# Linear attention and two mixer blocks in fp32 on one core: the main part of the first MLP taken from 288-token halves to block products over 256 and 512 tokens, with six early hidden tiles instead of five

## The chip, the core and the metric

The kernel runs on one core of a Trainium2 chip. The time is the device time of one execution in microseconds (us); of several runs the median is given. The engines are TensorE (PE; its loads of weights are PEld), VectorE (DVE), ScalarE (ACT), GpSimd (POOL) and SyncE (SP), whose queue issues the transfers (DMA). Each engine goes through its own instructions in order and waits for the others by semaphores.

## What is computed

Four batches of 576 tokens with 512 channels go through a linear attention with 8 heads and then through two mixer blocks:

```python
num = np.einsum('bhsf,bhfd->bhsd', q_p, kv)          # q_p, k_p = phi(q), phi(k)
x   = (num / den) as (batch, 576, 512)
u   = x + ((x.T @ U) @ V).T                          # mixing 1 over tokens, rank 32
x2  = u + relu(u @ w_ch1) @ w_ch2                    # first MLP, 512 -> 2048 -> 512
u2  = x2 + (relu(x2.T @ w_tok1) @ w_tok2).T          # mixing 2 over tokens, 576 -> 256 -> 576
out = u2 + relu(u2 @ w_m1) @ w_m2                    # second MLP, 512 -> 1536 -> 512
```

All of it is fp32. PE works on pairs of fp32r numbers: each operand is split into a high part (cast on ACT) and a low part (the difference, on DVE or POOL), and each product is the sum of three matmuls (high·high, high·low, low·high).

## The kernel before

The program has three stages, one after the other on PE, and the work around them overlaps.

The **attention stage** (to 394.8 us) goes through 16 groups of a batch and two heads in an order written out by hand (`rounds`, filled by `at`). Between them stand matmuls of the first MLP as a fill: NA = 5 of its 16 hidden tiles (a tile is 128 hidden channels), for 8 half batches of 288 tokens (hp_a is the first product, yp the second; their results go to DRAM as sD, u itself as uD). At its end come the mixing 1 of the last batch (rp, then mp) and the last halves' fill.

The **middle stage** (394.8 to about 741 us) does the other 11 hidden tiles for the same 8 halves (`channel`): per tile and half 12 matmuls of 288 columns into hp_b, a relu split (`relu_split`: hh on ACT, then hl on DVE), and two tiles later 12 matmuls into yb. The weights arrive as words of 64 bits that ACT and DVE decode (raw_b to w_b); the second MLP's words (raw_c) are decoded beside it and written back to DRAM as wD. After two halves follows `tokmix2`, mixing 2 of that batch: transposes x2p, the first product gp, a relu split (gh, gl), the second product m2p in four PSUM buffers. It is added to x2 in place and u2 goes to DRAM.

The **last stage** (from about 741 us) is the second MLP, 12 hidden tiles as 6 pairs, over token chunks c0 to c4 of 256, 512, 512, 512 and 512. c0 takes plain products. In the others `seven` computes a pair's first product as seven block products (Strassen's scheme, in Winograd's form): 2 × 2 blocks of the weights (sh, sl, 7 matrices, of which `sums` forms four) and of the tokens (`token_mats`, t0 to t6), 42 matmuls of 256 columns into PSUM tiles x, y, z, v instead of 48 of 512 columns at half the count. `second` then adds 24 matmuls of 512 columns a pair. x and y share two PSUM buffers (psh): x of the next pair waits until both readers of this pair's x are done. Its weights are loaded from wD, cast and split.

Of the kernel before, what the change touches and what calls it, by code (L numbers as in the profile page):

```python
# [19 lines left out]
P = 128  # L20
# [12 lines left out]
NA = 5  # L33
NR = NF2 - NA
# [4 lines left out]
READY = 8  # L39
FIRST = (4, 3, 5, 6, 2, 1, 0, 7, 8, 9, 10)  # L40
# [12 lines left out]
RAWX = 3  # L53
# [31 lines left out]
LAG = 2  # L85
O_WA = 4
D_WA = 5
# [8 lines left out]
def body(ctx, tc, kq, vd, w_phi, U, V, wm1, wt1, wt2, wm2, out):  # L96
# [32 lines left out]
    uD = [dr.tile([P, NC, N], F32, name=f"uD{i}") for i in range(2 * B)]  # L129
    sD = [dr.tile([P, NC, N], F32, name=f"sD{i}") for i in range(2 * B)]  # L130
# [230 lines left out]
    def split_tokens(xp, pool, nm, t):  # L361
        xh = pool.tile([P, C], F32R, tag="xh", name=f"xh{nm}")
        if t == 4:
# [101 lines left out]
    def tm2(b, ch):  # L465
# [10 lines left out]
        nc.sync.dma_start(uD[2 * b + ch], xT[:, :, sl])  # L476
# [56 lines left out]
    def ma_y(b, ch, c):  # L533
# [10 lines left out]
        if c == NC - 1:  # L544
            nc.sync.dma_start(sD[2 * b + ch], ys.pop((b, ch)))
# [76 lines left out]
    wB, begun = {}, []

    def load_next():
        f = FIRST[len(wB)]
        wB[f] = load_b(f)

    def half_next():
        f, k = FIRST[len(begun) // 2], len(begun) % 2
        if f >= NR:  # L630
            return
        begun.append(k)
        if k == 0:
            wB[f] = w_tiles(wrB[f], f"b{f}", f)
        load_half(wm1, NA + f, f"b{f}", k, *wB[f])
# [5 lines left out]
    while len(begun) < 2 * NR:  # L641
        half_next()
    while len(wB) < READY:
        load_next()
    PS.close()
    PB = ExitStack()
    psh = ctx.enter_context(tc.tile_pool(name="psh", bufs=2, space=PSUM, reuse_waits="tile"))
    psy = ctx.enter_context(tc.tile_pool(name="psy", bufs=1, space=PSUM, reuse_waits="tile"))
    psg = PB.enter_context(tc.tile_pool(name="psg", bufs=1, space=PSUM, reuse_waits="tile"))

    words = [(f, k) for p in range(NF2 // 2) for k in range(2) for f in (2 * p, 2 * p + 1)]

    def decode():
        f, k = words.pop(0)
        sl = slice(k * C, (k + 1) * C)
        nc.sync.dma_start(wD[f][:, sl], load64(wm2[f][:, sl], P, C, f"c{f}_{k}"))

    def channel(fs, uh, ul, xc, u, nm, pool=mlp):
        n = uh.shape[2]
        yp = [psy.tile([P, 512], F32, tag=f"y{c}", name=f"y{nm}_{c}") for c in range(NC)]  # L660
        nf = nB

        def second(f, hh, hl):
            wh, wl = wB[fs[f]]
            for c in range(NC):
                g = [(w2(wh, c), hh), (w2(wh, c), hl), (w2(wl, c), hh)]
                for i, (l, r) in enumerate(g):
                    mm(yp[c][:, :n], l, r, f == 0 and i == 0, f == nf - 1 and i == 2)

        waiting = []  # L670
        for f in range(nf):
            hp = h_tile(psh, wB[fs[f]], uh, ul, f"{nm}_{f}")
            hh, hl = h_pair(f, f"{nm}_{f}", pool, n)
            a, v = relu_split(hp[:, :n], hh, hl)
            if len(wB) < nB:
                with tc.issue_after(a), tc.issue_after(v):
                    load_next()
            elif nm != "b0_0" and f % 2 and words:
                with tc.issue_after(a), tc.issue_after(v):
                    decode()  # L680
            if f == nf - 3:
                with tc.issue_after(v):
                    nc.vector.tensor_add(xc, xc, u)
            if len(waiting) == LAG:
                second(*waiting.pop(0))
            waiting.append((f, hh, hl))
        for w in waiting:
            second(*w)
        for c in range(NC):
            nc.vector.tensor_add(xc[:, c], yp[c][:, :n], xc[:, c])  # L690

    def tokmix2(b, x2, T1H, T1L, T2H, T2L):
        gp = [psg.tile([P, C], F32, tag=f"g{j}", name=f"gp{b}_{j}") for j in range(2)]
        for t in range(NT):
            xp = psh.tile([P, C], F32, tag="m", name=f"x2p{b}_{t}")
            for c in range(NC):
                nc.tensor.transpose(xp[:, c * P : (c + 1) * P], token_tile(x2, c, t), ident)
            xh, xl = split_tokens(xp, b2, f"2{b}_{t}", t)
            for j in range(2):
                js = slice(j * P, (j + 1) * P)  # L700
                g = [(T1H[:, t, js], xh), (T1H[:, t, js], xl), (T1L[:, t, js], xh)]
                if xl is None:
                    del g[1]
                for i, (l, rr) in enumerate(g):
                    mm(gp[j], l, rr, t == 0 and i == 0, t == NT - 1 and i == len(g) - 1)
        gh = bc.tile([P, 2, C], F32R, tag="gh", name=f"gh{b}")
        gl = bc.tile([P, 2, C], F32R, tag="gl", name=f"gl{b}")
        for j in range(2):
            relu_split(gp[j], gh[:, j], gl[:, j])
        for ch in range(2):  # L710
            sl = slice(ch * N, (ch + 1) * N)
            for c in range(NC):
                cs = slice(c * P, (c + 1) * P)
                mp = psy.tile([P, 512], F32, tag=f"y{c}", name=f"m2p{b}_{ch}_{c}")
                g = []
                for j in range(2):
                    g += [(gh[:, j, cs], T2H[:, j, sl]), (gh[:, j, cs], T2L[:, j, sl]), (gl[:, j, cs], T2H[:, j, sl])]
                group(mp[:, :N], g)
                nc.vector.tensor_add(x2[:, c, sl], mp[:, :N], x2[:, c, sl])
            nc.sync.dma_start(u2D[:, :, b * S + ch * N : b * S + (ch + 1) * N], x2[:, :, sl])  # L720

    def load_u(src, nm):
        u = mlp.tile(list(src.shape), F32, tag="xT", name=f"u{nm}")
        nc.sync.dma_start(u, src)
        uh, ul = split_u(u, nm)
        return u, uh, ul

    def mix2_consts():
        T1H = bc.tile([P, NT, 256], F32R, name="T1H")
        T1L = bc.tile([P, NT, 256], F32R, name="T1L")  # L730
        for t in range(NT):
            w = load64(wt1[:, t], P, 256, f"t1_{t}")
            split(w, T1H[:, t], T1L[:, t], "v", "v")
        T2H = bc.tile([P, 2, S], F32R, tag="T2H", name="T2H")
        T2L = bc.tile([P, 2, S], F32R, tag="T2L", name="T2L")
        for j in range(2):
            for k in range(2):
                sl = slice(k * N, (k + 1) * N)
                w = load64(wt2[:, j, sl], P, N, f"t2_{j}_{k}")
                split(w, T2H[:, j, sl], T2L[:, j, sl], "v", "v")  # L740
        return T1H, T1L, T2H, T2L
# [295 lines left out]
```

## Time and profile before

| | |
|---|---|
| median of 3 runs (lowest to highest) | 1037.73 us (1037.57 to 1039.34) |
| the profiled execution | 1036.59 us, of which its span 1034.8 us |
| mean granted clock of TensorE | 0.995 |
| busy: PE, PEld, DVE, ACT, POOL | 98%, 91%, 59%, 43%, 20% |
| chain of work that ended last | PE 79%, DVE 9%, DMA 4%, ACT 3% |
| instructions | 17388, of them 6796 matmuls |

The span is the time from the first to the last instruction of the profiled execution. Busy shares are unions of the instructions' times. A matmul's own duration in the profile includes its way through the array, and successive ones overlap.

### The profile page before, as it was taken

What the parts mean: (1) busy time and instruction counts of PE and PEld (TensorE: products, weight loads), DVE (VectorE), ACT (ScalarE), POOL (GpSimd) and SP (SyncE); (2) the same over time, 40 slices, a digit from 0 to 9 for tenths busy, and PEclk for the clock granted to TensorE, in tenths of its full rate; (3) what the DMA queues carried; (4) which work ended last, traced back from release to release, by engine and by line L of the source; (5) the groups of instructions that cost most, each with busy time, mean ns of one, the idle gap of its engine ahead of it and who ended that gap; (6) DMA issues with size and microseconds to landing.
All of it is one profiled execution on the core that took longest, in us unless ns stands there. A gap on an engine that the chain in (4) does not pass through costs nothing.

```text
span 1034.8 us, 17388 instructions
## 1 busy us (share of the span) xinstructions
PE 1009.9 (98%) x6796; PEld 942.8 (91%) x6796; DVE 612.5 (59%) x1103; ACT 441.3 (43%) x1027; POOL 207.7 (20%) x166
## 2 busy tenths in 40 slices
PE   8998999999999899999999999999999999999998
PEld 6877899999999799999999999999899988898897
DVE  6676967776784767945444444326476753544533
ACT  6766665665655667532323232114342321222211
POOL 3111465566564234100000000005140000000000
PEclk9999999999999999999999999999999999999999
DMA  7454313232231675452632543202523030120201
GB/s 210 139 146 126 104 55 84 83 92 85 60 106 58 216 240 167 141 158 73 202 104 84 185 144 105 79 15 92 157 63 102 2 122 1 42 82 1 82 2 41
DMA packets 68514, 104.72 MB, mean 101 GB/s; under 512 B 17873, under 2 KB 42193, under 8 KB 68433
## 3 DMA queue, kind: packets, MB, share of 16 engines
q1 hardware_dynamic: 68432, 103.62, 32.5%
q8 instruction: 53, 0.87, 0.4%
q14 instruction: 29, 0.23, 0.1%
HBM read 78.28 MB, written 25.24 MB: 100 GB/s over the span
## 4 chain that ended last, share of the span: by engine, by line
PE 79%; DVE 9%; DMA 4%; ACT 3%; issue 2%; POOL 2%; SPq 0%; DVEq 0%; ACTq 0%; POOLq 0%
PE yc L114 15%; PE hp_b L114 11%; PE yb L114 11%; PE yp L114 5%; PE hp_a L114 5%; PE pp L114 4%; PE nm L114 4%; PE kvp L114 3%; PE vc L114 3%; PE xc L114 3%; PE zc L114 3%; PE gp L114 3%; PE m2p L114 2%; PE hpc L114 1%; DMA raw_a<-in_wm_dram 1%
## 5 line engine op out<-in xcount | busy, mean ns | idle before, releaser
L202 ACT ACTIVATE hhb<-hp_b 128x288 fp32r<-128x288 f32 x88 | 36.1, 410 | 174.8 <-PE hp_b L114 174.8
L114 PE MATMUL hp_b<-uhb,wh_b 128*128 128x288 f32 x352 | 103.9, 295 | 2.0 <-DVE hlb L203 2.0
L114 PE MATMUL hp_b<-uhb,wl_b 128*128 128x288 f32 x352 | 104.0, 296 | 0.0
L114 PE MATMUL hp_b<-ulb,wh_b 128*128 128x288 f32 x352 | 104.0, 295 | 0.0
L114 PE MATMUL yb<-hlb,wh_b 128*128 128x288 f32 x352 | 102.3, 296 | 0.0
L114 PE MATMUL yb<-hhb,wl_b 128*128 128x288 f32 x352 | 102.2, 295 | 0.0
L203 DVE SCALAR_TENSOR_TENSOR hlb<-hp_b,hhb 128x288 fp32r<-128x288 f32 x88 | 40.0, 456 | 103.4 <-ACT hhb L202 102.9
L114 PE MATMUL yb<-hhb,wh_b 128*128 128x288 f32 x352 | 94.7, 296 | 0.7 <-ACT hhb L202 0.7
L114 PE MATMUL yc<-hlc,vh 128*128 128x512 f32 (+1 forms) x240 | 88.9, 373 | 0.0
L114 PE MATMUL yc<-hhc,vl 128*128 128x512 f32 (+1 forms) x240 | 88.9, 373 | 0.0
L114 PE MATMUL pp<-KW,kq 128*128 128x256 f32 x320 | 83.1, 385 | 2.4 <-PE kvt L344 1.3
L107 POOL TENSOR_TENSOR sl<-w_c,sh 128x256 fp32r<-128x256 f32 (+1 forms) x18 | 20.3, 1151 | 311.9 <-ACT sh L102 307.0
L114 PE MATMUL yc<-hhc,vh 128*128 128x512 f32 (+1 forms) x240 | 81.5, 373 | 0.0
L114 PEld LDWEIGHTS hp_b<-uhb,wh_b 128*128 128x128 f32 x352 | 66.2, 188 | 2.7 <-DVE hlb L203 2.5
L295 DVE TENSOR_REDUCE km<-pp 128x4 f32<-128x512 f32 x80 | 54.7, 685 | 23.4 <-PE pp L114 22.9
L114 PEld LDWEIGHTS pp<-KW,kq 128*128 128x128 f32 x320 | 57.1, 191 | 10.5 <-PE kvt L344 1.7
L114 PEld LDWEIGHTS hp_b<-ulb,wh_b 128*128 128x128 f32 x352 | 66.2, 188 | 0.3
L114 PEld LDWEIGHTS yb<-hlb,wh_b 128*128 128x128 f32 x352 | 66.2, 188 | 0.0
L114 PEld LDWEIGHTS yb<-hhb,wl_b 128*128 128x128 f32 x352 | 66.2, 188 | 0.0
L114 PEld LDWEIGHTS hp_b<-uhb,wl_b 128*128 128x128 f32 x352 | 66.1, 188 | 0.0
L107 POOL TENSOR_TENSOR qel<-qe,qeh 128x640 fp32r<-128x640 f32 (+1 forms) x40 | 59.9, 1511 | 27.2 <-DVE qeh L104 17.7
L114 PEld LDWEIGHTS yb<-hhb,wh_b 128*128 128x128 f32 x352 | 63.1, 188 | 1.0 <-ACT hhb L202 0.9
(243 smaller groups left out, 2820.1 us busy)
## 6 DMA issues: line engine op xcount, KB each, us to landing
raw_c<-in_wm_dram SPq DMA_DIRECT2D x24, 512.0 KB, 4.4
raw_b<-in_wm_dram SPq DMA_DIRECT2D x22, 512.0 KB, 4.7
kq<-in_kq_dram SPq DMA_DIRECT2D x80, 128.0 KB, 2.4
wD<-w_c SPq DMA_DIRECT2D x24, 256.0 KB, 2.2
w_c<-wD SPq DMA_DIRECT2D x24, 256.0 KB, 3.4
raw_a<-in_wm_dram SPq DMA_DIRECT2D x10, 512.0 KB, 4.4
rec<-rD SPq DMA_DIRECT2D x32, 144.0 KB, 3.3
uD<-xT SPq DMA_DIRECT2D x8, 576.0 KB, 4.4
```

Source lines behind the costliest of these rows:

```text
L107: return ENG[e].tensor_tensor(out=o, in0=a, in1=b, op=ALU.subtract)
L114: return nc.tensor.matmul(o, l, r, start=start, stop=stop, skip_group_check=True)
L202: a = nc.scalar.activation(hh, hp, AF.Relu)
L203: v = nc.vector.scalar_tensor_tensor(out=hl, in0=hp, scalar=0.0, in1=f32(hh), op0=ALU.max, op1=ALU.subtract)
L295: nc.vector.tensor_reduce(out=m, in_=pv, op=ALU.max, axis=AX.X, apply_absolute_value=True)
```

## The change

The attention stage gets a sixth early hidden tile (NA = 6). The middle stage takes the last stage's code: `channel`, `seven`, `second` and `token_mats` serve both, with `st` "b" or "c". For b it is 10 hidden tiles in 5 pairs over chunks b0 (256 tokens, plain) and b1 to b4 (512, seven products). Both stages share one memory plan: the weight pairs' pools `wp`, the token tiles, and a ring of 4 slots for the hidden tiles and the mixing's tiles. Four pairs of weights are loaded at the end of the attention stage (`half_next`, now with two raw buffers instead of five), the fifth in b0's first pairs. What else is to be done is hung behind pairs by `hooksB` and `hooksC`: the sums of the weights, mixing 2's matrices, the decoding of the second MLP's words. u, its early sums and x2 go through DRAM tensors u1D, s1D and x2D; in each b chunk u is read a second time and added to `res` at pair 1 (line 820). Mixing 2 comes later: of batch 0 after b2, 1 after b3, 2 after b4 and after the loads of the second MLP's first five pairs, 3 inside c0, behind its pair 1 (`flush`). m2p now shares the two psh buffers. The t1 and t5 splits and the splits of mixing 2's matrices go to POOL.

```diff
-NA = 5
+NA = 6
...
-RAWX = 3
...
-D_WA = 5
+D_WA = 4
...
+    def half_next():
+        p, k, i = halves.pop(0)
+        if p not in wB:
+            wB[p] = pair_tiles(p, "b")
+        w = load64(wm1[NA + 2 * p + i][:, k * C : (k + 1) * C], P, C, f"b{2 * p + i}_{k}")
+        put_half(w, wB[p], k, i, "p")
...
-            split(src, t[:, 0], t[:, 1], "a", "v")
+            split(src, t[:, 0], t[:, 1], "a", "vpvvvpv"[i])
...
+    def channel(st, i, sl_, W, np_, src, plain, hooks):
...
+        for p in range(np_):
+            hs, r = one(p) if plain else seven(p)
...
+            for fn in hooks.get(p, ()):
+                with tc.issue_after(r[0]), tc.issue_after(r[1]):
+                    fn()
+            if p == 1 and st == "b":
+                u_ = pu.tile([P, NC, 2 * HM], F32, tag="u", name=f"v{nm}")[:, :, :n]
+                nc.sync.dma_start(u_, src[:, :, sl_])
+                with tc.issue_after(r[1]):
+                    nc.vector.tensor_add(res, res, u_)
+            if waiting:
+                second(*waiting.pop(0))
+            waiting.append((p, hs))
+            if p == 1 and "flush" in hooks:
+                second(*waiting.pop(0))
+                hooks["flush"]()
...
-                mp = psy.tile([P, 512], F32, tag=f"y{c}", name=f"m2p{b}_{ch}_{c}")
+                mp = psh.tile([P, 512], F32, tag="m", name=f"m2p{b}_{ch}_{c}")
...
+    slots = [("w", 2)] * 2 + [("r", 2)] * 2 + [("raw", RAWB)] * 2
...
+    hooksB = [
+        {0: [half_b], 1: [half_b], 2: [sums_b(0)], 3: [sums_b(1)]},
+        {0: [sums_b(2)], 1: [sums_b(3)], 2: [sums_b(4)], 3: t1[:2], 4: t1[2:4]},
+        {0: t1[4:] + t2[:1], 1: t2[1:], 2: dd, 3: dd, 4: dd},
+        {p: dd for p in range(NB)},
+        {0: dd, 1: dd, 2: dd, 3: dd},
+    ]
+    for i, sl in enumerate(spans):
+        channel("b", i, sl, wB.__getitem__, NB, u1D, i == 0, hooksB[i])
...
+        if i >= 2:
+            mix2_load(i - 2)
+            if i < 4:
+                tokmix2(i - 2)
+    for p in range(NB):
+        weights_c(p)
+    tokmix2(2)
+    mix2_load(3)
```

How this moves instructions shows at three places. The first is PE at the end of the attention stage, around the last matmul of mixing 1's first product (rp) and its second product (mp); yp is the fill. Before:

```order
1349 L114 MATMUL yp_1_3_4658<-hla_1_4_4591,wh_a_922 128x288
1350 L114 MATMUL yp_1_3_4658<-hha_1_4_4590,wl_a_923 128x288
1351 L114 MATMUL rp_4282<-xh_4_4332,US 128x512
1352 L114 MATMUL mp_0_0_4340<-VS,rh_4336 128x288
1353 L114 MATMUL mp_0_1_4344<-VS,rh_4336 128x288
```

And now:

```order
1471 L113 MATMUL yp_1_2_4819<-hha_1_5_4762,wl_a_932 128x288
1472 L113 MATMUL rp_4406<-xh_4_4456,US 128x512
1473 L113 MATMUL yp_1_3_4839<-hha_1_0_4617,wh_a_240 128x288
1474 L113 MATMUL yp_1_3_4839<-hla_1_0_4618,wh_a_240 128x288
...
1490 L113 MATMUL yp_1_3_4839<-hha_1_5_4762,wl_a_932 128x288
1491 L113 MATMUL mp_0_0_4464<-VS,rh_4460 128x288
1492 L113 MATMUL mp_0_1_4468<-VS,rh_4460 128x288
```

The 18 matmuls of the last yp stand between rp and mp, where there was nothing.

The second place is DVE between pairs 1 and 2 of a chunk whose pairs also carry `sums`. Here are chunk c1 before, and b1 now (s3 are pieces of the sums of pair 3; hl, u2 and x are the pair's tiles; res and v are the residual and the u read again).

```order
840 L203 SCALAR_TENSOR_TENSOR hlc1_1_1_9529<-hbc1_1_9502,hhc1_1_1_9528 128x512
841 L816 TENSOR_TENSOR s3_0_9536<-sh3_8900,sl3_8901 128x512
842 L816 TENSOR_TENSOR s3_1_9537<-sh3_8900,sl3_8901 128x256 x2
843 L929 TENSOR_TENSOR u2c1_2_9608<-yc1_2_9579,ec1_2_9588 128x256
844 L203 SCALAR_TENSOR_TENSOR hlc1_1_0_9527<-hac1_1_9524,hhc1_1_0_9526 128x256
845 L203 SCALAR_TENSOR_TENSOR hlc1_2_0_9635<-xc1_2_9578,hhc1_2_0_9634 128x256
```

```order
L199 SCALAR_TENSOR_TENSOR hlb1_1_1_5946<-hbb1_1_5919,hhb1_1_1_5945 128x512
L678 TENSOR_TENSOR s3_0_5953<-sh_b3_5135,sl_b3_5136 128x512
L678 TENSOR_TENSOR s3_1_5954<-sh_b3_5135,sl_b3_5136 128x256 x2
L820 TENSOR_TENSOR resb1_5797<-resb1_5797,vb1_5971 128x2048
L784 TENSOR_TENSOR u2b1_2_6028<-yb1_2_5999,eb1_2_6008 128x256
L199 SCALAR_TENSOR_TENSOR hlb1_1_0_5944<-hab1_1_5941,hhb1_1_0_5943 128x256
L199 SCALAR_TENSOR_TENSOR hlb1_2_0_6055<-xb1_2_5998,hhb1_2_0_6054 128x256
```

The add of 2048 columns stands inside the row of DVE's work of which x of pair 2 is the last; x of pair 3 waits for that last row.

The third place is PE in the mixing 2 of batch 0, between its two products. Before:

```order
2179 L114 MATMUL gp_1_6003<-xh_4_6069,T1H 128x512
2180 L114 MATMUL gp_1_6003<-xh_4_6069,T1L 128x512
2181 L114 MATMUL hp_b_0_1_6177<-uhb_0_6151,wh_b_4910 128x288
2182 L114 MATMUL hp_b_0_1_6177<-ulb_0_6152,wh_b_4910 128x288
...
2202 L114 MATMUL hp_b_0_2_6203<-uhb_0_6151,wh_b_4808 128x288
2203 L114 MATMUL m2p_0_0_6082<-T2H,gh_6076 128x288
```

And now:

```order
2591 L113 MATMUL gp_1_6964<-hhx_4_7030,T1H 128x512
2592 L113 MATMUL gp_1_6964<-hhx_4_7030,T1L 128x512
2593 L113 MATMUL m2p_0_0_7046<-T2H,hhg_0_7038 128x288
2594 L113 MATMUL m2p_0_0_7046<-T2L,hhg_0_7038 128x288
2597 L113 MATMUL m2p_0_0_7046<-T2H,hlg_0_7039 128x288
```

The 22 matmuls of the next half between gp and m2p are gone from there.

## Rows read from the trace of the kernel before

**Rows 1.** The page: each engine's busy time, share of the span, instructions.

```profile
PE 1009.9 (98%) x6796; PEld 942.8 (91%) x6796; DVE 612.5 (59%) x1103; ACT 441.3 (43%) x1027; POOL 207.7 (20%) x166
```

**Rows 2.** Three stretches: length, each engine's busy time (instructions), clock, DMA share, GB/s.

```profile
0.00:394.80 394.80, 378.31 (x2429) 346.52 (x2430) 284.60 (x470) 250.36 (x624) 166.28 (x133) 0.99 0.40 121
394.80:741.00 346.20, 342.02 (x2489) 333.47 (x2489) 174.24 (x305) 116.89 (x239) 29.20 (x22) 1.00 0.39 122
741.00:1034.00 293.00, 289.58 (x1882) 262.82 (x1881) 153.67 (x329) 74.06 (x166) 12.20 (x11) 1.00 0.15 50
```

**Rows 3.** Undisturbed stretches of one form or mix of matmuls, columns as before.

```profile
500.00:550.00 50.00, 50.00 (x379) 50.00 (x378) 23.30 (x38) 15.68 (x32) 0.00 (x0) 1.00 0.48 144
752.00:770.00 18.00, 17.62 (x149) 17.41 (x149) 14.56 (x25) 9.29 (x23) 9.26 (x9) 1.00 0.20 58
840.00:900.00 60.00, 60.00 (x375) 53.74 (x375) 29.03 (x60) 14.19 (x30) 0.00 (x0) 1.00 0.13 46
```

**Rows 4.** End of the attention stage: two stretches, and PE's timeline there.

```profile
350.00:358.00 8.00, 6.25 (x37) 4.98 (x35) 6.43 (x13) 4.86 (x11) 2.98 (x3) 1.00 0.57 174
358.00:366.00 8.00, 6.19 (x26) 5.71 (x25) 5.03 (x8) 3.79 (x5) 1.19 (x1) 0.58 0.99 308
354.43 0.79 PE L114 MATMUL mp<-VS,rh 128*128 128x288 f32 x4 [1.25 <-ACT rh L102]
360.70 0.61 PE L114 MATMUL hp_a<-ula,wh_a 128*128 128x288 f32 x1 [0.80 <-DVE ula L107]
```

**Rows 5.** The middle stage's start, and the way into the last stage.

```profile
394.80:430.00 35.20, 33.17 (x247) 32.70 (x247) 29.48 (x52) 23.64 (x53) 12.74 (x9) 1.00 0.52 163
430.00:470.00 40.00, 39.06 (x293) 38.50 (x292) 23.31 (x47) 14.47 (x28) 0.00 (x0) 1.00 0.48 141
728.00:750.00 22.00, 21.27 (x149) 19.45 (x148) 10.21 (x19) 7.79 (x15) 2.22 (x2) 1.00 0.45 142
```

**Rows 6.** Groups by form: DVE in 394.8 to 741 us, POOL over all.

```profile
L163 DVE SCALAR_TENSOR_TENSOR w_c<-w_c,r_c 128x512 int32<-128x512 int32 x24 | 16.6, 692 | 15.1 <-ACT r_c L161 15.1
L683 DVE TENSOR_TENSOR x<-x,ub 128x1152 f32<-128x1152 f32 x8 | 11.5, 1441 | 0.0
L163 DVE SCALAR_TENSOR_TENSOR w_b<-w_b,r_b 128x512 int32<-128x512 int32 x8 | 7.4, 931 | 4.2 <-ACT w_b L160 4.1
L107 POOL TENSOR_TENSOR wl_b<-w_b,wh_b 128x512 fp32r<-128x512 f32 x22 | 30.4, 1386 | 59.5 <-ACT wh_b L102 56.5 <-PE yp L114 2.9
```

**Rows 7.** Timelines of DVE and PE in chunk c1: start us, us.

```profile
794.10 0.69 DVE L203 SCALAR_TENSOR_TENSOR hlc<-hbc,hhc 128x512 fp32r<-128x512 f32 x1
794.71 1.36 DVE L816 TENSOR_TENSOR s<-sh,sl 128x512 f32<-128x512 f32 x3
796.32 0.42 DVE L203 SCALAR_TENSOR_TENSOR hlc<-hac,hhc 128x256 fp32r<-128x256 f32 x1
796.65 0.42 DVE L203 SCALAR_TENSOR_TENSOR hlc<-xc,hhc 128x256 fp32r<-128x256 f32 x1
...
796.24 1.09 PE L114 MATMUL yc<-hhc,vh 128*128 128x512 f32 x4
797.17 0.40 PE L114 MATMUL xc<-t0c,sh 128*128 128x256 f32 x2
```

**Rows 8.** The tile gh: ns of one (least, median, most), first and last start.

```profile
L202 ACT ACTIVATE gh<-gp x8: 592/594/602, 479.3 to 737.9; 128x512 fp32r<-128x512 f32 x8
L203 DVE SCALAR_TENSOR_TENSOR gl<-gp,gh x8: 680/686/692, 480.0 to 738.7; 128x512 fp32r<-128x512 f32 x8
```

**Rows 9.** The tile w_c's casts, and transfers: KB each, us to landing.

```profile
L102 ACT CAST sh<-w_c x18: 398/402/622, 704.2 to 755.2; 128x256 fp32r<-128x256 f32 x12, 128x512 fp32r<-128x512 f32 x6
w_c<-wD SPq DMA_DIRECT2D x24, 256.0 KB, 3.4
u2D<-x SPq DMA_DIRECT2D x8, 576.0 KB, 3.6
uc<-u2D SPq DMA_DIRECT2D x4, 1024.0 KB, 5.4
```

More of the change, by code (lines that the diff above doesn't have):

```diff
@@ L640, in body @@
                 fn(*args)
-    while len(begun) < 2 * NR:
+    while halves and halves[0][0] in wp:
         half_next()
-    while len(wB) < READY:
-        load_next()
     PS.close()
-    PB = ExitStack()
+    AB.close()
     psh = ctx.enter_context(tc.tile_pool(name="psh", bufs=2, space=PSUM, reuse_waits="tile"))
     psy = ctx.enter_context(tc.tile_pool(name="psy", bufs=1, space=PSUM, reuse_waits="tile"))
-    psg = PB.enter_context(tc.tile_pool(name="psg", bufs=1, space=PSUM, reuse_waits="tile"))
@@ L722, in load_u @@
[L722 to L741, printed above, removed]
@@ L767, in body @@
-    slots = [(stc, "w", 4)] * 4 + [(stc, "raw", RAWB)] * 2
-    more = [(pt, t, 1) for t in ("t1", "t3", "t4")]
-    def loadc(f, j, p):
-        if p >= 2 and more:
-            slots.extend(more)
-            more.clear()
-        pool, tag, bufs = slots.pop(0)
-        slots.append((pool, tag, bufs))
-        w = pool.tile([P, 512], F32, tag=tag, name=f"w_c{f}_{j}", bufs=bufs)
-        nc.sync.dma_start(w, wD[f][:, j * C : (j + 1) * C])
-        return w
-    def sums3(p, wa, wb, sh, sl):
-        t = wc[0].tile([P, 512], F32, tag="s", name=f"s{p}")
-        a, b = t[:, :256], t[:, 256:]
-        def tt(o, x, y, op, i):
-            nc.vector.tensor_tensor(out=o, in0=x, in1=y, op=op)
-            split(o, sh[:, i], sl[:, i], "a", "v")
-        tt(a, wb[:, :256], wb[:, 256:], ALU.add, 3)
-        tt(b, a, wa[:, 0], ALU.subtract, 4)
-        tt(a, wa[:, 0], wb[:, :256], ALU.subtract, 5)
@@ L807, in body @@
-    wC = [pair_weights(p) for p in range(NF2 // 2)]
-    def sums(p):
-        sh, sl = wC[p][:2]
+    psc = ctx.enter_context(tc.tile_pool(name="psc", bufs=1, space=PSUM, reuse_waits="tile"))
+    pt = ctx.enter_context(tc.tile_pool(name="pt", **right))
+    pc = ctx.enter_context(tc.tile_pool(name="pc", **right))
+    wp[NB - 1] = ctx.enter_context(tc.tile_pool(name=f"wp{NB - 1}", **right))
+    TX = ExitStack()
+    tx = TX.enter_context(tc.tile_pool(name="tx", **right))
+    words = [(f, k) for p in range(NCP) for k in range(2) for f in (2 * p, 2 * p + 1)]
@@ L956, in second @@
                     for k, (l, r) in enumerate(g):
-                        mm(yp[c][:, :n], l, r, p == 0 and i == 0 and k == 0, p == NF2 // 2 - 1 and i == 1 and k == 2)
-        prev = None
-        for p in range(NF2 // 2):
-            hs = one(p) if plain else seven(p)
-            if plain and p < EARLY:
-                sums(p)
-            if prev is not None:
-                second(*prev)
-            prev = (p, hs)
-        second(*prev)
-        for c in range(NC):
-            nc.vector.tensor_add(res[c], yp[c][:, :n], res[c])
-            nc.sync.dma_start(out[:, c, sl_], res[c])
@@ new lines, in channel, with mix2_t1 @@
+        if waiting:
+            second(*waiting.pop(0))
+        for c in range(NC):
+            nc.vector.tensor_add(res[:, c], yp[c][:, :n], res[:, c])
+            nc.sync.dma_start((x2D if st == "b" else out)[:, c, sl_], res[:, c])
+    T = {}
+    def mix2_t1(t):
+        if not T:
+            T["1"] = [tx.tile([P, NT, 256], F32R, name=f"T1{x}") for x in "HL"]
+            T["2"] = [tx.tile([P, 2, S], F32R, name=f"T2{x}") for x in "HL"]
+        w = load64(wt1[:, t], P, 256, f"t1_{t}")
+        split(w, T["1"][0][:, t], T["1"][1][:, t], "a", "p")
@@ new lines, in half_b, with sums_b, sums_c, loadc @@
+    def half_b():
+        half_next()
+        half_next()
+    def sums_b(p):
+        return lambda: sums(p, wB[p])
+    def sums_c(p):
+        return lambda: sums(p, wC[p])
+    slots = [("w", 2)] * 2 + [("r", 2)] * 2 + [("raw", RAWB)] * 2
+    def loadc(f, j):
+        tag, bufs = slots.pop(0)
+        slots.append((tag, bufs))
+        w = stage.tile([P, 512], F32, tag=tag, name=f"w_c{f}_{j}", bufs=bufs)
+        nc.sync.dma_start(w, wD[f][:, j * C : (j + 1) * C])
+        return w
+    def weights_c(p):
+        wC[p] = pair_tiles(p, "c")
+        for k in range(2):
+            for i in range(2):
+                put_half(loadc(2 * p + i, k), wC[p], k, i, "pv"[i])
```

310 lines of the change are left out of this document (133 added, 177 removed).

## The prediction

> **What bounds the kernel now.** I read the page first: TensorE (PE) is busy for 1009.9 us, 98% of the span [rows 1]. The table of three stretches then gives each stage its share: the attention stage idles PE for 16.5 us of 394.8, the main part of the first MLP for 4.2 of 346.2, the last stage for 3.4 of 293 [rows 2]. VectorE (DVE) stands at 72%, 50% and 52% there, GpSimd (POOL) at 29.2 us in the middle stretch. So time goes mostly where matmuls go, and a change that takes matmuls out pays unless it makes PE wait.
>
> A matmul's price is not its duration, since they overlap, but the pace at which they follow one another. In 50 undisturbed microseconds 379 matmuls of 288 columns are touched, two cut by the edges: 133 ns each. Between 752 and 770 us only 256-column ones run: 17.62 us for 149, 118 ns. From 840 to 900 us 374 (375, less a cut one) mix in the pattern of a pair, 42 of 256 and 24 of 512: a pair takes 60/374×66 = 10.59 us, less 42×0.118 is 5.6 us, 234 ns for 512 columns [rows 3].
>
> **The matmuls.** Removed: 8 half batches × 11 hidden tiles × 24 = 2112 of 288 columns, ×0.133 = 280.9 us. Added: chunk b0, plain, 10 tiles × 24 = 240 of 256 columns, 28.3 us; four chunks × 5 pairs × 42 = 840 of 256, 99.1 us, and × 24 = 480 of 512, 112.3 us: 239.8 us. The sixth early tile adds 8 × 24 = 192 of 288 columns in the attention stage, 25.5 us. The token mixings and the second MLP keep their matmuls. **Sum −15.6 us.** The rest is waits.
>
> **End of the attention stage: −2.** Before, PE waits 1.25 us for the copy of rp, soon runs into more waits of the next fill matmuls (one of 0.80 us), and then its granted clock falls: 0.58 in the mean over 358 to 366 us, the lower level, 1.2 GHz, in most of it, with 26 matmuls in 8 us where 60 of 133 ns fit [rows 4]. The order shows 18 yp matmuls (2.4 us) between the last rp and the first mp now, so the 1.25 us is covered. The later waits stay. If the clock then holds, the 22 or so matmuls at half pace (6.19 us busy for 26, 0.24 each instead of 0.133) give some 2.4 us back too; if the added loads through only two raw buffers disturb this stretch, up to 5 us are lost. Ends −5 and +5; I take −2, the covered wait and a part of the clock.
>
> **Start of the middle stage: −1, then +1.** PE is idle 2.0 us in 394.8 to 430 and 0.9 in 430 to 470 [rows 5], the weights still being decoded beside the first half batches. Afterwards four of five pairs are loaded before the stage, and the fifth's four halves in its first two pairs: some 5 us to land, by the 1 MB transfer's 5.4 [rows 9], and some 6 us of work, against 22.6 us (192 matmuls of 118 ns) until PE wants it. I take the later 0.9 us (with some of what follows) as gone, −1, and keep the first 2.0. In b0 DVE has two sets of sums, the splits for b1 and pair 5's decoding: 26 us at the pace of its starts (0.33 us for 256 columns, 0.61 for 512 [rows 7]) against PE's 28.3. That little margin costs nothing to 3; I take +1.
>
> **The add of u in b1: +2.2.** Line 820 adds 128x2048 elements. 0.33 and 0.61 us for 256 and 512 columns give 1.08 ns a column, so 2.3 us; the 1152-column add took 1441 ns in the mean [rows 6], which fits. The order puts it between the pieces of a pair's sums and the two splits behind them. In chunk c1, the same code before, that spot has no slack: the split of xc starts at 796.65 and takes 0.42, and the next xc matmul starts at 797.17, exactly when the yc ahead of it (796.24 on) are through [rows 7]. So in b1 the x of pair 3 comes 2.2 us late, and everything behind it. In b2, b3 and b4 PE has some 20 matmuls of `second` (4.7 us) ahead of that x in the order, and no sums run beside: nothing there. Ends 0 and 5 (b1 and b2).
>
> **The mixings: +2.5.** Between the last gp and the first m2p stand a relu on ACT, 0.59 us, and a split on DVE, 0.69 [rows 8]. Before, ten hp matmuls (1.3 us) of the next half lie between. After, m2p follows gp directly: 0.6 to 0.8 us bare for each of four. Ends 2 and 5. That m2p has two PSUM buffers instead of four is free: a group of 6×0.133 = 0.8 us covers the add of 0.46.
>
> **Into the last stage: +3.** 20 pieces of weights are loaded, cast and split while b4 ends and mixing 2 runs. From b4's last z to the m2p PE has 22 us of work, DVE 15 us by its starts with POOL idle. With POOL busy DVE stretches: the same two-input integer operation took 931 ns on w_b (POOL busy) and 692 on w_c (POOL idle) [rows 6]. The splits of x2p, which PE needs, stand in DVE's order behind splits that wait for a load. Least: nothing. Most: the pieces of weights come at the pace of before, 51.0 us for 24 (704.2 to 755.2), 2.1 us each [rows 9]; begun 7 us ahead, the 18th is there at 31 us, 9 too late. Nearer is the low end, since six slots of some 6 us (3.4 landing, cast, split) give one each 1 us: +3. Mixing 3 loads x_3 only when the stores of x_2 are through: 0.5 for the add, 3.6 for the store, then 1.15 MB, by the 5.4 us of 1 MB an estimated 6.1 [rows 9], 10.2 together, against 88 matmuls of c0 (10.4 us): +1. What is lost there now, 0.7 us [rows 5], goes: net +3. In c0, sums and pair 6's splits fill DVE to about PE's own time: +0.5 (0 to 3).
>
> **Sum:** −15.6−2−1+1+2.2+2.5+3+0.5 = −9.4 us. The profiled execution took 1036.6 us (1.8 around its span), 1.1 below the median of the three runs, 1037.7; on the median, **1028 us**.
>
> **Rivals.** *Covers hold everywhere* (0.25): only the bare mixings (2.5) and half the add (1.1) stay: −15.6−2−1+3.6 = −15.0, 1023 us. For it: PE idles for 0.0 us in all of c1 to c4, the very code that now runs in B. Against it: c1 has no slack.
>
> *The last stage's weights come late* (0.13), the side that is slower. If they come 2.1 us apart and only once the last decoded word is stored, the 18th arrives at 38 us against 22: 16 us instead of 3, 1041 us. It decides from a wait of 12.5 us on. For it: those loads share SP's queue with stores that wait for DVE. Against it: six slots.
>
> *DVE and POOL shut each other out* (0.10). If a two-input DVE operation had to wait for a whole POOL split (1386 ns [rows 6]), then the t1 and t5 splits, which are POOL's now, would cost up to 4×1.4 us in the pairs without slack (b1 and c1), and ten splits of weights at the entry to the last stage 4 more, where 7 us of slack take the rest: 1037 or 1038 us, no change. The row shows a mean of 0.24 us, a sixth of a POOL split, for each DVE operation beside it: a share of it. The Trainium skill's page "SBUF — State Buffer" (section "Who interferes with whom") says just this: a VectorE instruction with two SBUF inputs and a GpSimd one that reads SBUF take an exclusive lock, and the loser waits for the whole instruction. By that rule taken strictly the sum would be this rival's; by the row it is the 3 us above.
>
> *The early tile costs more* (0.07): PE's idle at the end of the attention stage stays, the clock falls once more behind a new wait (2.4 us again): −9.4+2+2.4+2 more of loads, 1035 us.
>
> **How the numbers follow.** My forecast holds 0.45, with its own range 1024 to 1033 from the bounds above. Runs of one kernel here lie within about 0.2% (2 us), so that is what counts as no change. Faster: 0.45, 0.25, 0.07 and half of the lock's 0.10, 0.82. Same: the other half, 0.05. Slower: 0.13. The range 1020 to 1038 leaves out the late weights and little more.
>
> **What would show it.** Matmuls: PE's count falls by 2112−1752 = 360 (a few records can lack), its busy time by 13 to 16 us. End of the attention stage: no wait at the first mp; the granted clock between 340 and 400 us tells the rest. b1: PE waits some 2 us for a DVE split at x of pair 3, right behind the 2048-column add. Mixings: four waits of m2p for ACT and DVE, 0.6 us each. Entry to the last stage: DVE's splits of x2p waiting behind splits of weights; if PE idles there more than 12 us, I am wrong in sign. Chunks b2 to b4 should run as c2 to c4 do, with 10.6 us a pair; if their pairs take longer, the decoding of the second MLP's weights between them is what I have missed.

## The result, and the profile after

The changed kernel takes 1053.26 us (median of 4 runs, 1050.73 to 1056.77); the kernel before, on the same chip, 1038.53 (1037.57 to 1040.15). The ratio is 1.0143, with a 95% interval of 1.0109 to 1.0176: slower by 15 us, where I had forecast 1028 us and faster. It lies outside the range.

The page of the changed kernel: the span, and the engines' busy time, share and instructions, to be read beside [rows 1].

```profile
span 1050.5 us, 16980 instructions
PE 1003.8 (96%) x6436; PEld 907.8 (86%) x6436; DVE 677.5 (64%) x1251; ACT 461.0 (44%) x1091; POOL 230.4 (22%) x184
```

PE has the 360 matmuls less that were forecast, and is busy 6 us less in a span 15.7 us longer. The next table has the stretches of the changed kernel: the three stages, as in [rows 2], and then places that the text below comes to (length; busy time and instructions of PE, PEld, DVE, ACT, POOL; granted clock; DMA share; GB/s).

```profile
0.00:429.00 429.00, 404.17 (x2621) 371.01 (x2622) 294.62 (x486) 256.59 (x643) 172.73 (x142) 0.99 0.37 111
429.00:741.00 312.00, 295.36 (x1849) 260.85 (x1848) 221.21 (x420) 127.92 (x277) 39.55 (x32) 0.99 0.55 179
741.00:1050.00 309.00, 304.30 (x1972) 275.93 (x1970) 161.71 (x346) 76.53 (x172) 18.16 (x10) 1.00 0.15 50
50.00:100.00 50.00, 39.99 (x173) 30.14 (x172) 36.63 (x67) 32.29 (x89) 8.75 (x7) 0.93 0.51 142
625.00:650.00 25.00, 20.68 (x121) 17.48 (x120) 17.71 (x29) 12.29 (x24) 3.00 (x2) 1.00 0.41 112
712.00:741.00 29.00, 23.25 (x120) 17.71 (x119) 22.06 (x36) 13.70 (x29) 10.55 (x8) 1.00 0.83 268
```

The middle stage idles PE for 16.6 us of 312, where it was 4.2 of 346. DVE's share there went from 50% to 71% (221.21 of 312). The last stage from c1 on is as it was: 257.8 us to the end, before 258.3.

A wait is one part of a loss; matmuls that follow each other slowly are the other. So I worked out, for every matmul, the time to the start of the next one less its undisturbed pace (133, 118 and 234 ns [rows 3], 109 for 128 columns and 147 for 320; 216 and 269 for the attention stage's own fp32 products of 256 and 320), and summed it by stretch. Here and in the experiments, "lost" is this sum, in us:

| lost time of PE | before | after | change | forecast |
|---|---|---|---|---|
| first 100 us | 14.5 | 22.8 | +8.3 | 0 |
| from there to the last 60 us of the attention stage | 6.6 | 5.5 | −1.1 | 0 |
| last 60 us of the attention stage | 9.4 | 11.0 | +1.6 | −2 |
| first 75 us of the middle stage (b0, b1's add) | 3.9 | 8.1 | +4.2 | +2.2 |
| middle stage to 25 us before c0 | 1.3 | 12.9 | +11.6 | +1.2 |
| those 25 us and c0 | 1.8 | 9.3 | +7.5 | +4.8 |
| sum | 37.5 | 69.6 | +32.1 | +6.2 |

With the matmuls' −15.6 that makes +16.5, against 15.7 in the spans. So the forecast of the matmuls holds, and the error is all in the waits: 26 us more than forecast, 19 of them in the two rows that I had put at nothing or almost nothing. Most of the middle stage's loss lies at two places: 6.1 us from x of b3's last pair to x of b4's first (625 to 665 us, with the mixing of batch 1 between), and 9.2 from x of b4's last pair to c0 (699 to 741 us); the last 6.2 of these belong to the row below.

What ended PE's longer waits in the middle stage of the changed kernel (total us, times, longest):

```profile
PE yb L113 <- DVE hlb L199: 3.2, 2, 2.2
PE hpb L113 <- DVE hlb L199: 3.1, 2, 2.9
PE m2p L113 <- ACT hhg L198: 1.6, 4, 0.7
PE gp L113 <- DVE hab L793: 1.5, 1, 1.5
PE gp L113 <- ACT hhx L367: 1.5, 1, 1.5
PE xb L113 <- ACT eb L101: 1.3, 3, 0.6
PE xb L113 <- DVE u2b L784: 1.2, 1, 1.2
PE gp L113 <- DVE hlx L106: 1.2, 1, 1.2
```

No single wait is large, and nearly all are for short DVE and ACT operations that stand in a queue behind something else.

### The profile page after: what moved, and what is told of

Its sections match the earlier page's. It is cut to its first block, busy times and chain, and to the rows that moved or that the text cites. A ratio compares the mean times of both kernels' runs of the same rounds, so it can differ in the third digit from the quotient of the medians.

```text
span 1050.5 us, 16980 instructions
## 1 busy us (share of the span) xinstructions
PE 1003.8 (96%) x6436; PEld 907.8 (86%) x6436; DVE 677.5 (64%) x1251; ACT 461.0 (44%) x1091; POOL 230.4 (22%) x184
## 5 line engine op out<-in xcount | busy, mean ns | idle before, releaser
L113 PE MATMUL yc<-hlc,vh_c 128*128 128x512 f32 (+1 forms) x240 | 88.0, 372 | 0.0
L113 PE MATMUL yc<-hhc,vl_c 128*128 128x512 f32 (+1 forms) x240 | 87.9, 372 | 0.0
L113 PE MATMUL yc<-hhc,vh_c 128*128 128x512 f32 (+1 forms) x240 | 78.5, 372 | 0.0
L113 PE MATMUL yb<-hlb,vh_b 128*128 128x512 f32 (+1 forms) x200 | 74.8, 376 | 3.2 <-DVE hlb L199 3.2
L113 PE MATMUL yb<-hhb,vl_b 128*128 128x512 f32 (+1 forms) x200 | 74.4, 374 | 0.0
L113 PE MATMUL yb<-hhb,vh_b 128*128 128x512 f32 (+1 forms) x200 | 64.2, 376 | 0.9 <-ACT hhb L198 0.7
L113 PE MATMUL hp_a<-ula,wh_a 128*128 128x288 f32 x192 | 57.8, 301 | 2.1 <-DVE ula L106 2.1
L113 PE MATMUL hp_a<-uha,wh_a 128*128 128x288 f32 x192 | 58.1, 306 | 1.3 <-ACT uha L101 1.0
L113 PE MATMUL yp<-hha,wh_a 128*128 128x288 f32 x192 | 57.6, 303 | 0.7 <-ACT hha L198 0.7
L113 PE MATMUL hp_a<-uha,wl_a 128*128 128x288 f32 x192 | 57.7, 301 | 0.0
```

The source lines that it names most:

```text
L113: return nc.tensor.matmul(o, l, r, start=start, stop=stop, skip_group_check=True)
```

## The experiments

Theories, from the table. **A:** the first 100 us lose time because the early weights, 12 pieces instead of 10, are fetched closer together: two in 4 rounds instead of two in 5. **L:** the token splits t1 and t5 and the weights' splits on POOL hold up single DVE operations (the rival that I had given 0.10). **D:** the second MLP's decoding, moved beside the seven-product pairs, makes DVE and ACT late. **R:** two raw buffers instead of five disturb the attention stage. **T:** the sixth tile itself costs there. **F:** it is not the decoding's work, but that its transfers are fetched too late.

A ratio compares a run with the kernel before on the same chip, where its median was 1038.5 to 1039.6 us. Differences in us between an experiment and the changed kernel's 1053.26 compare medians from different times and mostly different chips, and the interval of the changed kernel is itself some 3.5 us wide to either side.

**e1, A.** The spacing of the early fetches back in the changed kernel:

```diff
-D_WA = 4
+D_WA = 5
```

> The changed kernel with the early tiles' words fetched every 2.5 rounds again (D_WA 5) instead of every 2. Theory A, the denser loads crowd the attention stage's start (PE idle 22.8 us in its first 100 us, 14.5 before): 5 to 8 us faster, the loss in the first 100 us back near 15. Rival, the start varies by itself: within 2 us, the loss stays near 22.

Measured: 1049.17 us, ratio 1.0095 [1.0075, 1.0115]; lost in the first 100 us 16.7 instead of 22.8. The stretch of 50 to 100 us, first row above, is now:

```profile
50.00:100.00 50.00, 45.84 (x216) 36.12 (x213) 39.60 (x74) 34.48 (x93) 7.68 (x6) 0.97 0.54 150
```

216 matmuls against 173. PE's waits there, first of the changed kernel and then of e1:

```profile
PE kvt L340 <- ACT kvT L101: 5.9, 3, 2.5
PE pp L113 <- issue: 3.4, 2, 2.3
PE nm L113 <- ACT KH L101: 2.2, 1, 2.2
```

```profile
PE kvt L340 <- ACT kvT L101: 5.3, 2, 2.8
...
PE pp L113 <- issue: 1.3, 1, 1.3
```

The wait of nm for a cast on ACT and one of pp are gone, and the granted clock is 0.97 instead of 0.93. A holds, for 6 us of that stretch; e6 and e8 below, at 15.3 and 21.1, bear it out. The whole kernel gained 4.1 us by the medians, less than expected, and the intervals of the two ratios overlap slightly. In the profiled execution the middle stage to 25 us before c0 lost 17.3 us instead of 12.9, with its code untouched (e4, e10 and e14, which leave it alone too, lost 12.6, 15.4 and 12.7), so differences of 4 us in that row alone show nothing.

**e2 and e15, L.** e2 puts all of POOL's splits of the middle and last stage on DVE, e15 only t1 and t5:

```diff
-            split(src, t[:, 0], t[:, 1], "a", "vpvvvpv"[i])
+            split(src, t[:, 0], t[:, 1], "a", "v")
```

> The changed kernel with every split that POOL does for the middle and last stage (weights, t1, t5, mixing 2's matrices) on DVE instead. Theory L, DVE operations that stretch from 0.68 to 1.78 us beside a POOL split make PE wait: 5 to 9 us faster, no stretched DVE operation after 350 us, less PE idle at 450, 632 and 712 to 741 us. Rival D, it is DVE's amount of work: 10 pieces more of 0.6 us at the entry to the last stage and 0.6 us for each other split, the same time or up to 6 us slower.

> The changed kernel with the t1 and t5 splits on DVE, as all seven were in the kernel before; POOL keeps the weights and the matrices of mixing 2. Theory L, of the gain of all splits on DVE (5.4 us) the token splits make most: 2 to 4 us faster. Rival, the weights' splits at the end of the attention stage make it: under 1 us.

Measured: e2 1047.90 us, 1.0087 [1.0065, 1.0109]; e15 1047.69 us, 1.0076 [1.0057, 1.0094]. How, shows in the timelines of the last pair of b3, beside which the tokens of b4 are split. The changed kernel (start us, us, engine, line, operation; in brackets the idle time ahead and what ended it):

```profile
630.55 0.68 DVE L106 TENSOR_TENSOR t0b<-ub,t0b 128x512 fp32r<-128x512 f32 x1
631.05 1.33 POOL L106 TENSOR_TENSOR t5b<-ub,t5b 128x512 fp32r<-128x512 f32 x1 [65.90 <-ACT t5b L101]
631.15 1.77 DVE L162 SCALAR_TENSOR_TENSOR w_c<-raw_c,w_c 128x512 int32<-128x512 int32 x1
632.35 1.69 POOL L106 TENSOR_TENSOR t1b<-ub,t1b 128x512 fp32r<-128x512 f32 x1
632.85 1.48 DVE L199 SCALAR_TENSOR_TENSOR hlb<-hab,hhb 128x256 fp32r<-128x256 f32 x1
634.38 0.50 PE L113 MATMUL yb<-hlb,vh_b 128*128 128x512 f32 x1 [2.23 <-DVE hlb L199]
```

and e15, the same operations:

```profile
629.47 0.68 DVE L106 TENSOR_TENSOR t0b<-ub,t0b 128x512 fp32r<-128x512 f32 x1
630.06 0.68 DVE L162 SCALAR_TENSOR_TENSOR w_c<-raw_c,w_c 128x512 int32<-128x512 int32 x1
630.67 0.42 DVE L199 SCALAR_TENSOR_TENSOR hlb<-hab,hhb 128x256 fp32r<-128x256 f32 x1
...
631.34 0.68 DVE L106 TENSOR_TENSOR t5b<-ub,t5b 128x512 fp32r<-128x512 f32 x1
```

A DVE operation of 0.68 us that begins just behind a POOL split ends 0.54 us after it, 1.77 us long; the next, of 0.42, takes 1.48, and PE waits 2.23 us. Two splits of 0.68 us more on DVE cost less than two on POOL beside it: from x of b3's last pair to x of b4's first, e15 and e2 lose 2.5 us instead of 6.1. PE idles 0.65 us there in e15, with the whole decoding in place:

```profile
625.00:650.00 25.00, 24.35 (x134) 20.28 (x133) 20.36 (x38) 13.45 (x26) 0.00 (x0) 1.00 0.52 159
```

L holds, for 5.6 us by the medians. e2, with more splits off POOL, gains no more than e15.

**e3, D.** Half of the decoding left out:

```diff
-    words = [(f, k) for p in range(NCP) for k in range(2) for f in (2 * p, 2 * p + 1)]
+    words = [(f, k) for p in range(NCP // 2) for k in range(2) for f in (2 * p, 2 * p + 1)]
...
-        nc.sync.dma_start(w, wD[f][:, j * C : (j + 1) * C])
+        nc.sync.dma_start(w, wD[f % 6][:, j * C : (j + 1) * C])
```

> The changed kernel decodes only half of the second MLP's words (12 of 24 pieces; the other half of the weights is loaded from the first six tiles' again: that part of the computation is changed). Theory D, DVE's queue stands behind words that have not landed (b3 and b4 carry two pieces a pair): 3 to 6 us faster, PE's idle of 5.2 us in 625 to 650 us mostly gone. Rival L (POOL's splits stretch DVE): under 2 us, since t1 and t5 stay where they are.

Measured: 1041.82 us, 1.0024 [1.0014, 1.0035], 11.4 us less than the changed kernel; lost from 75 us into the middle stage to c0's end 13.2 instead of 22.2. The stretch of 625 to 650 us of e3, with twelve pieces left out:

```profile
625.00:650.00 25.00, 25.00 (x147) 21.84 (x146) 16.38 (x28) 9.70 (x18) 2.63 (x2) 1.00 0.29 97
```

PE has no idle time left, with the two POOL splits still there. They still hold DVE up, but what PE waits for is already through:

```profile
629.29 0.42 DVE L199 SCALAR_TENSOR_TENSOR hlb<-hab,hhb 128x256 fp32r<-128x256 f32 x1
629.96 1.65 DVE L704 TENSOR_TENSOR ub<-ub,ttb 128x512 f32<-128x512 f32 x1
631.53 1.77 DVE L106 TENSOR_TENSOR t3b<-ttb,t3b 128x512 fp32r<-128x512 f32 x1
```

So the stall at the end of b3 needs both, a piece's decoding ahead of hlb and the splits on POOL, and the gains of e3 and e15 cannot be added. Nor are e3's 11.4 us the decoding alone. From x of b3's last pair to x of b4's first it loses 0.8 us instead of 6.1, where pieces are missing. From x of b4's last pair to c0 it loses 4.3 instead of 9.2, but there the loads of the last stage's weights also begin at 617.3 us instead of 703.4, so that they no longer stand together behind the last pieces; e14 below, which keeps the decoding and leaves out most of those weights, loses 4.2. The edit takes out the operations and the transfers together, so F was still possible.

**e9, F.** Each piece fetched one hook ahead of its decoding:

```diff
-    dd = [decode, decode]
+    dd = [decode, decode, fetch, fetch]
```

> The changed kernel, but the second MLP's words are fetched one pair ahead of the pair that decodes them (two raw buffers as they are). Theory F, ACT and DVE stand at words that have not landed (5.1 us after a fetch in the same pair), and PE behind them: 4 to 8 us faster, of the 12.9 us that PE idles in the rest of the middle stage 5 to 7 gone. Rival, it is the decoding's work itself on DVE: within 2 us, since the work stays.

Measured: 1053.41 us, 1.0162 [1.0114, 1.021]; lost in the middle of the stage 12.9, as in the changed kernel. From x of b3's last pair to x of b4's first it loses 6.0 instead of 6.1, though ACT waits for no piece between 602 and 675 us. F falls as the cause of that stall: with the transfer early, the same operations still stand in the queues.

**e13 and e16, D by place.** The mixing's matrices and the decoding in fewer pairs, away from the last two pairs of b3 and b4:

```diff
-        {0: [sums_b(2)], 1: [sums_b(3)], 2: [sums_b(4)], 3: t1[:2], 4: t1[2:4]},
-        {0: t1[4:] + t2[:1], 1: t2[1:], 2: dd, 3: dd, 4: dd},
-        {p: dd for p in range(NB)},
-        {0: dd, 1: dd, 2: dd, 3: dd},
+        {0: [sums_b(2)], 1: [sums_b(3)], 2: [sums_b(4)], 3: t1[:3], 4: t1[3:]},
+        {0: t2, 1: dd, 2: dd, 3: dd, 4: dd},
+        {0: dd, 1: dd + dd, 2: dd},
+        {0: dd, 1: dd + dd, 2: dd},
```

e16 adds the edits of e1 and e15, and line 820 at pair 3.

> The changed kernel with the same 24 pieces of words decoded, but none beside a chunk's last two pairs and the mixing behind them in b3 and b4 (eight pieces each in b2 pairs 1 to 4, b3 pairs 0 to 2, b4 pairs 0 to 2). Theory P, DVE and ACT go through the decoding in order just where the mixing and the next chunk's token splits are urgent: 4 to 7 us faster, PE's idle of 5.2 us around the mixing of batch 1 down to 2. Rival, the amount of decoding work counts wherever it stands: within 2 us.

> What the single changes suggest together: early words every 2.5 rounds, the decoding away from the mixings, t1 and t5 on DVE, the second reading of u added at pair 3 of b1 to b4 instead of pair 1. If the causes add up: 12 to 16 us faster than the changed kernel, 1037 to 1041 us, no better than the kernel before. If the decoding's placement is a miss: 6 to 9 us.

Measured: e13 1064.85 us, 1.0239 [1.0217, 1.0261]; e16 1058.20 us, 1.0181 [1.016, 1.0203]. The placement makes it worse. e13's waits of PE in the middle stage:

```profile
PE gp L113 <- ACT hhx L367: 8.4, 3, 7.1
PE vb L113 <- DVE hbb L791: 5.9, 4, 2.8
PE gp L113 <- DVE hlx L106: 3.3, 2, 2.6
```

The waits of the old place are gone: the end of b3 loses 2.6 us instead of 6.1. New ones stand elsewhere; gp waits 7.1 us, since on ACT the casts of the last stage's weights, which wait for their loads, come ahead of hhx. But this is no clean test of the place. With up to four pieces in a pair and two raw buffers to land in, ACT waits far longer for pieces that have not landed. These are its waits in the changed kernel, in e9 and in e13 (total us, times, longest):

```profile
ACT w_c L156 <- DMA raw_c<-in_wm_dram: 9.7, 7, 3.3
ACT w_c L156 <- DMA raw_c<-in_wm_dram: 5.8, 2, 2.9
ACT w_c L156 <- DMA raw_c<-in_wm_dram: 43.2, 16, 7.2
```

In e16 they are 30.6 us. So e13 and e16 show that this placement is worse, and do not show that the decoding costs the same wherever it stands; the same pieces spread otherwise, or with more buffers, were not tried.

**e5, e6, e7 and e8: the parts in the kernel before.** e5 has D_WA = 4; e6 a sixth early tile (NA = 6, READY = 7 and an order of the halves without the sixth); e7 two raw buffers; e8 all three.

```diff
-NA = 5
+NA = 6
...
-        pool = stage if len(halves) % (RAWB + RAWX) < RAWB or not extra else extra[0]
+        pool = stage
```

> The kernel before with its ten early pieces of words fetched every 2 rounds (D_WA 4). Theory A, denser early loads crowd the attention stage's start: 4 to 8 us slower, lost in the first 100 us. Rival: within 2 us.

> The kernel before with six early tiles and ten in the middle stage (D_WA stays 5, five raw buffers stay). The matmuls are the same in number, only moved. Theory T, the sixth tile by itself loads the attention stage's end: 4 to 8 us slower. Rival: within 2 us, and the loss of the changed kernel's attention stage comes from the raw buffers and the fetches.

> The kernel before with two raw buffers throughout instead of five at the end of the attention stage. Theory R, with two buffers ACT and DVE stand at words that have not landed, and PE behind them: 3 to 6 us slower, lost between 336 and 430 us. Rival: within 2 us.

> The kernel before with all three at once: six early tiles, D_WA 4, two raw buffers; the attention stage of the changed kernel in front of the middle stage of before. If these three make the changed kernel's attention stage, 8 to 11 us slower; if not, less than 4.

| | us | ratio | lost, first 100 us | lost, last 60 us of attention |
|---|---|---|---|---|
| e5 | 1040.76 | 1.0024 [1.001, 1.0038] | 16.0 | 9.9 |
| e6 | 1031.49 | 0.9933 [0.9919, 0.9948] | 15.3 | 4.0 |
| e7 | 1050.91 | 1.0125 [1.0105, 1.0146] | 14.5 | 14.1 |
| e8 | 1047.66 | 1.0085 [1.0066, 1.0104] | 21.1 | 8.3 |

T falls, with the other sign: the tile gains 7 us. The last 60 us of e6's attention stage run at full clock:

```profile
353.40:413.40 60.00, 56.94 (x414) 55.31 (x415) 39.18 (x58) 36.28 (x70) 17.56 (x13) 1.00 0.61 208
```

R holds in the kernel before, for 12 us, twice what was expected, of which 4.7 are lost in the last 60 us of the attention stage and the rest mostly behind it. e8's first 100 us are those of the changed kernel, where twelve pieces, two in 4 rounds, lose 6.6 us more than the kernel before; ten at that spacing (e5) lose 1.5 more and twelve at the wider one (e6) 0.8: it takes both.

**e10, R in the changed kernel.** Three more raw buffers for the last twelve pieces, borrowed from token tiles (t5, t6 and u) that are free until b1:

```diff
+        if extra and k >= 2:
+            raw = extra[0].tile([P, 512], I64, tag=("t5", "t6", "u")[k - 2], name=f"raw_{name}")[:, :n]
```

> The changed kernel, but twelve of the late weight pieces land in five raw buffers: the third to fifth lie in the token tiles t5, t6 and u, which stand empty until b0. Theory R (two raw buffers in the new memory plan): the idle of PE in the attention stage's last 60 us falls from 11.0 to 5 and that of b0 by 1 to 3, 6 to 9 us faster. Rival T (the sixth tile's fill itself runs into DVE): within 3 us.

Measured: 1060.28 us, 1.0201 [1.0168, 1.0233]; lost at the end of the attention stage 11.2, as in the changed kernel (11.0), and in the first 35 us of the middle stage 11.0 instead of 6.5. The buffers did not help. They hardly took away what they were meant to: the engines still idle 11.7 us for these pieces to land, against 13.6 in the changed kernel. So whether R costs anything in the changed kernel stays open.

**e4 and e14, the entry to the last stage.** Weights of pairs 1 to 4 left out, their matmuls reading those of pair 0 (e4: `wC[p] = wC[0]`), or those of the middle stage:

```diff
-    for p in range(NB):
-        weights_c(p)
+    weights_c(0)
+    for p in range(1, NB):
+        wC[p] = wB[p]
```

> The changed kernel loads, casts and splits the second MLP's weights for pair 0 and pair 5 only; pairs 1 to 4 use pair 0's tiles (that part of the computation is changed), so 16 of 20 pieces fall away at the entry to the last stage. Theory W, the pieces hold DVE's queue there (PE idle 8.6 us in 712 to 741 us): 5 to 8 us faster, that idle down to 2 or 3. Rival M, the bare mixing and the stores before the next load make it: under 3 us.

> The changed kernel without the loads, casts and splits of the second MLP's pairs 1 to 4, which use the first MLP's tiles as they stand (that part of the computation is changed); no tile is shared by two pairs here. Theory W, these 16 pieces hold DVE, ACT and POOL at the entry to the last stage: 4 to 7 us faster, PE's idle of the 25 us before the last stage down from 6.2 to 3 or less. Rival M, the mixing's own chain makes it: under 2 us.

Measured: e4 1069.05 us, 1.0293 [1.0269, 1.0317]. It is inconclusive: five pairs on one set of tiles made c0 itself lose 16.2 us. e14: 1048.46 us, 1.0086 [1.0065, 1.0107]; lost in the 25 us before c0 and in c0 6.3 instead of 9.3. So the loads, casts and splits of 16 pieces are worth 3 us there, and 5 counted from x of b4's last pair on (4.2 instead of 9.2), near the 4.8 by the medians.

**e11 and e12, together.** e11 has the edits of e1, e9 and e10; e12 also those of e2.

> Three repairs at once: early words every 2.5 rounds, five raw buffers at the end of the attention stage, the second MLP's words fetched a pair ahead. If the causes are separate, the sum of the single ones, 14 to 20 us faster than the changed kernel: 1034 to 1039 us. If they hide one another (a wait that only moves), 8 to 12 us.

> The three repairs, and all splits of the middle and last stage on DVE instead of POOL. Theory L (a DVE operation stands while POOL splits): 3 to 6 us faster than the three alone, 1030 to 1034 us. Rival D: the added DVE work at the entry to the last stage eats it, the same within 2 us.

Measured: e11 1050.96 us, 1.0111 [1.0089, 1.0134]; e12 1044.14 us, 1.0045 [1.0027, 1.0063]. e11 gained 2.3 us where at least 8 were expected, since e9 and e10 had no gain to add. Between the two stand the POOL splits alone: 6.8 us, L once more. No version of the change beat the kernel before. The fastest kernel here is e6, the kernel before with the sixth early tile: 1031.49 us.

## Why the prediction was wrong

**The matmuls, −15.6: right.** 360 fewer, and table and spans agree within 1 us.

**The decoding of the second MLP: the step that failed.** I costed it at nothing. The pairs of b2 to b4 were to run like those of c2 to c4, and the middle of the stage, for which 1.2 us were forecast, lost 11.6 more. Its 24 pieces were decoded from 438 to 628 us before, beside plain tiles with DVE half idle, and now from 548 to 705, beside pairs that want DVE for every block sum. The busy shares that I read do not say who stands behind whom: an operation that waits for a piece, or is one too many ahead of a split, makes PE wait while DVE is at 71%. I had named it as what would be missed if the pairs of b2 to b4 took longer than those of c2 to c4, but gave it neither a term nor a rival. With half of it left out the kernel is 11.4 us faster (e3): the stall of 6.1 us at the end of b3 goes, and some 5 us at the entry to the last stage, where pieces are missing and the last stage's weights also load earlier, so that the two are not told apart. An earlier fetch does not take the stall away (e9). POOL's splits have to come together with the decoding for it (e15). Which of the decoding's parts, its operations on ACT, those on DVE or its stores in SP's queue, costs most was not separated.

**"DVE and POOL shut each other out": the rival that was right in its mechanism.** I priced a DVE operation beside a POOL split at a sixth of the split, from a mean of 931 against 692 ns [rows 6]. Means were the wrong view. One that gives the least, the median and the most ns of a tile's operations shows it, here of w_b in the kernel before, where it could have been read, in the changed kernel, and in e2, without the POOL splits:

```profile
L166 DVE SCALAR_TENSOR_TENSOR w_b<-raw_b,w_b x22: 676/692/1719, 344.1 to 417.7; 128x512 int32<-128x512 int32 x22
```

```profile
L162 DVE SCALAR_TENSOR_TENSOR w_b<-raw_b,w_b x20: 676/693/1760, 356.5 to 444.6; 128x512 int32<-128x512 int32 x20
```

```profile
L162 DVE SCALAR_TENSOR_TENSOR w_b<-raw_b,w_b x20: 676/684/693, 356.7 to 442.1; 128x512 int32<-128x512 int32 x20
```

With the splits on POOL, at least half of the operations are undisturbed and the longest is over 1 us longer: a whole wait for some, nothing for others. The Trainium skill's page "SBUF — State Buffer" (section "Who interferes with whom") has a DVE instruction with two SBUF inputs contend with a GpSimd one that reads SBUF, under an exclusive lock; the trace agrees (1.77 us at 631 us, ended 0.54 us after the split). e15 prices it at 5.6 us, and the rival had up to 4×1.4 for the same splits, but that the two agree is luck: the rival had them in b1 and c1, where e15 keeps the only wait of b1 (1.2 us, behind the add) and c1 to c4 lose nothing in either, and the stall is at the end of b3.

**"End of the attention stage: −2": right in one wait, wrong in the sum.** The wait of the first mp is covered as forecast, 0.4 us instead of the 1.25 of [rows 4], and e6 shows that the tile gains more than I gave it: 5.4 us lost less at the end of the stage, the clock held. But I charged nothing for fetching more weights more closely at the start (6 us, e1). The bound of 5 for the two raw buffers fits that stretch in the kernel before, where e7 loses 4.7 more; but e7 costs 12.4 in all, and for the other stretches I had no term. Why the changed kernel's last 60 us still lose 11.0 is settled in part: e2, with w_b's splits off POOL, loses 7.0 there, but 1.8 more ahead of it. The rest is open, since e10 left most of the waits for the pieces in place. Open too is why the closer spacing costs with twelve pieces and hardly with ten (e5, e8).

**The start of the middle stage, +1 −1, and the add of u, +2.2: the add right in kind and put too high, the start too low.** The add takes 2.29 us, as forecast, but PE waits only 1.24 behind it:

```profile
482.53 2.29 DVE L820 TENSOR_TENSOR resb<-resb,vb 128x2048 f32<-128x2048 f32 x1
484.73 0.42 DVE L784 TENSOR_TENSOR u2b<-yb,eb 128x256 f32<-128x256 f32 x1
...
485.20 0.51 PE L113 MATMUL xb<-t0b,sh_b 128*128 128x256 f32 x2 [1.24 <-DVE u2b L784]
```

(By the starts a column costs 1.09 ns, not 1.08; the 2.3 us stand.) The rest of the 4.2 us is in b0, where I saw little margin and gave it 1: at 454.1 us hpb waits 2.92 us for hlb. Two POOL splits at 447 and 448.6 us stretch two DVE operations ahead of that hlb from 0.68 to 1.78 us each, but they are not the reason, since e2, with no split of this stage on POOL, has nearly the same wait:

```profile
PE hpb L113 <- DVE hlb L199: 2.7, 1, 2.7
```

There DVE does those splits itself; either way hlb stands in DVE's order behind the token splits of b1 and the sums.

**The mixings, +2.5: right in size.** Of the three mixings in the middle stage m2p waits 1.6 us for hhg, 0.7 at most at a time, where 0.6 to 0.8 each were forecast.

**Into the last stage, +3 and +0.5: mechanism right, size too low.** With its mixings 4.8 us were forecast, 7.5 came; the weights are 3 of them (e14, 5 with the last pair of b4), and gp's waits for hab, hhx and hlx (1.5, 1.5, 1.2 us) show what I had named, short operations behind the weights' casts and splits. The rival with 16 us of it did not come.

## What to carry to other kernels

Before you move side work beside another stage, ask for every operation of it which operations of the critical engine's suppliers will stand behind it in the same in-order queue; a supplier at 50 to 70% busy is no cover. Where two engines may block each other, read the least, median and longest duration of one operation, since a mean turns a few full waits into a small tax on all. And try the parts of a change one by one in the old kernel: here one of them, the sixth tile, was faster than either kernel.

## What the runs showed of the hardware

The start of the kernel is sensitive to how close the prefetches stand: twelve fetches of 512 KB at two in 4 rounds instead of two in 5 cost 6 us (e1; 5.8 between e6 and e8), with a granted clock of 0.93 instead of 0.97 in the mean over 50 to 100 us (e1). And a GpSimd split can cost more than it takes off DVE: two of them, some 1.5 us each on POOL, held up two DVE operations by 1.1 us each, where DVE does them itself in 0.68 us apiece.
